# Attention ahead of an expert layer: the gate's product in another set of PSUM banks, the gate's parts one unit later, keys handed to the DMA queue ahead of values

## The chip, the core and the metric

The kernel runs on one core of a Trainium2 chip. The metric is the device time of one execution in microseconds (us). Before the change three runs took 722.42, 722.44 and 722.80 us, median 722.44. The profile shown here is of one further execution, of 717.54 us.

## The reference

Two layers in one kernel. First attention, in 8 batches of 8 heads with 512 local and 32 global positions of width 64: a local query sees the 32 global keys and the local keys at most 32 positions away, a global query sees all 544 keys. Then a mixture of experts over the 4608 resulting rows of 512 numbers, where each of 8 experts takes 576 rows.

```
s_g = scale * q_g @ k_all.T ;  out_g = softmax(s_g) @ v_all
s_l = scale * q_l @ [k_g, k_l].T, local part masked to |i - j| <= 32
out_l = softmax(s_l) @ [v_g, v_l]
x = concat(out_g, out_l) as rows of H * D = 512
logits = x @ w_gate          # 4608 x 8
walk over all (row, expert) in falling order of logits;
    a row goes to the expert if it has none yet and the expert has < 576
out[rows of e] = relu(x[rows] @ w1[e]) @ w2[e]
```

## The kernel before, in words

**Stages.** Attention comes first, then the first expert's choice of its rows (a chain of small steps, nothing beside it), then the eight experts' products, beside which the other experts' choices are made.

**Units.** Attention is a list of 80 units, ten a batch. Two heads make a pair; a batch has pairs 0 to 3, over all batches 0 to 31. A pair has two `Local` units; two pairs together have one `Glob` unit. In batches 0 to 6 the units are four Local, one Glob, four Local, one Glob. In batch 7 they are two Local, both Glob, six Local, so that the second Glob (units[73]) needs the keys of pair 31.

**Steps of a unit.** `a` (L164, L230) multiplies queries and keys into PSUM tile `S` (three banks). `e` masks and takes row maxima on VectorE (DVE, L171, L173) and exponentials on ScalarE (ACT, L176). `c` transposes on TensorE (PE, L181, L259) into PSUM tile `T` (three banks), and `evac` copies the result to SBUF, on ACT (L289) or DVE (L291) by a fixed turn of five. `d` multiplies with the values into PSUM tile `O` (two banks: L193, L269), and DVE divides (L196 to L202, L272 to L276) into the batch's rows `xs` or `xg`. That makes eight banks.

**Order.** The scheduler is off; each engine runs in the order of the code. Step i of the main loop does `c` of unit i, `a` and `e` of unit i+2, `d` of unit i-2. At an even step the order is a, c, gate parts, e, d; at an odd step d, c, gate parts, a, e. So the `d` of an even step and that of the odd step after it come close together.

**Gate.** The logits of batch b are made during the next batch, in six parts: four times four transposes into a T bank (`gate_x`, L297), one product with the gate's weights into an O bank (`gate_m`, L303, placed straight behind `d`), whose result is copied to `ltc`, and four transposes of that into a T bank with a sum on DVE (`gate_l`, L312, L313). The table `GS` gives the steps, counted from an even one. Batches 3 and 7 have another, smaller gate for the global rows.

**DMA queue.** All attention loads and stores go through SyncE's queue (SP) in program order. `slot`, called twice a step, issues one of: a load of a pair's queries and keys (`load_qk`: `q` 272 KB, then `qk` 432 KB), half a pair's values (`load_v`, 520 KB), a store of a quarter of a batch's rows (`stores`, 256 KB), ahead of which the small stores of a Glob's rows go (`late`, four of 8 KB). Ahead of each stands a DMA of four bytes (`pace`) that reads a result of DVE, so the queue cannot run ahead of the computation. A load of keys comes up when its pair is at most three past that of the unit two steps ahead. GpSimd (POOL) copies `q` into the padded tile `qz` (L87), from which `a` reads.

**First choice.** `rt.setup` for the first 24 columns of logits is spread over the last steps of attention, one piece a step, from step nu - 9 on (nu = 80).

Of the kernel before, what the change touches and what calls it, by code (L numbers as in the profile page):

```python
# [8 lines left out]
F32 = mybir.dt.float32  # L9
# [30 lines left out]
@with_exitstack  # L40
def block(ctx, tc, A, out, nbatch=B, dump=None):
    nc = tc.nc
    ctx.enter_context(tc.manual_schedule())
    consts = ctx.enter_context(tc.tile_pool(name="consts", bufs=1))
    dram = ctx.enter_context(tc.tile_pool(name="dram", bufs=1, space=DRAM))
    xd = dram.tile([N, DM], F32, name="xd")
    pace = dram.tile([1, 256], F32, name="pace")

    ident = consts.tile([128, 128], F32, name="ident")
    L = consts.tile([128, 34, E], F32, name="L")  # L50
    if dump is not None:
        nc.vector.memset(L, 0.0)
    rt = Routing(tc, A, consts, L, ident) if out is not None else None
    if rt:
        rt.begin(ctx)
    attention(tc, A, consts, xd, pace, ident, L, nbatch, rt)
    if dump is not None:
        nc.sync.dma_start(dump["L"], L.rearrange("p a b -> p (a b)"))
        nc.sync.dma_start(dump["x"][:nbatch * S], xd[:nbatch * S])
    if out is not None:  # L60
        rt.begin_ps(ctx)
        experts(tc, A, xd, ident, rt, out)
# [3 lines left out]
def attention(ctx, tc, A, consts, xd, pace, ident, L, nbatch, rt=None):  # L66
    nc = tc.nc
# [3 lines left out]
    ps = ctx.enter_context(tc.tile_pool(name="ps", bufs=2, space=PSUM))  # L71
# [4 lines left out]
    def load_qk(b, p):  # L76
        t = ld.tile([128, KW], F32, name="qk", bufs=5)
        q = ld.tile([128, QW], F32, name="q", bufs=3)
        z = qz[(b * NP + p) % NZ]
        nc.sync.dma_start(q, A["qk"][b, p, :, :QW])  # L80
        nc.sync.dma_start(t, A["qk"][b, p, :, QW:])
        qk[b, p] = t

        def spread(eng):
            for h in range(2):
                r = slice(64 * h, 64 * h + 64)
                eng.tensor_copy(z[r, :, h, :], q[r].rearrange("p (j i) -> p j i", i=32))  # L87
        return spread

    def load_v(b, p, h=None):  # L90
        if not h:
            vw[b, p] = ld.tile([128, 2, NW, D + 1], F32, name="vw", bufs=6)
        t = vw[b, p].rearrange("p h w d -> p (h w d)")
        n = NW * (D + 1)
        q = slice(0, 2 * n) if h is None else slice(h * n, h * n + n)
        nc.sync.dma_start(t[:, q], A["vw"][b, p, :, q])
# [5 lines left out]
    P = [(b, p) for b in range(nbatch) for p in range(NP)]  # L102
# [20 lines left out]
    seen, late, stores = [], [], []  # L123
    nl = [3, 4]
    npace = [0]

    def behind():
        nc.sync.dma_start(pace[:, npace[0]:npace[0] + 1], seen[-1])
        npace[0] += 1

    def slot(i):
        v = nl[1] < 2 * nl[0]
        k = not v and nl[0] < len(P) and nl[0] <= pairidx(units[min(max(i, 0) + LA, nu - 1)]) + 3
        if not (v or k or late or stores):
            return
        if i >= 0 and seen:
            behind()
        while late:
            late.pop(0)()
        if stores and (len(stores) > 2 or not v):  # L140
            stores.pop(0)()
        elif v:
            load_v(*P[nl[1] // 2], nl[1] % 2)
            nl[1] += 1
        elif k:
            load_qk(*P[nl[0]])(nc.gpsimd)
            nl[0] += 1

    class Local:
        def __init__(s, b, u):  # L150
# [135 lines left out]
    def evac(dst, src, act=None):  # L286
        nev[0] += 1
        if nev[0] % 5 < 3 if act is None else act:
            nc.scalar.activation(dst, src, AF.Copy)  # L289
        else:  # L290
            nc.vector.tensor_copy(dst, src)  # L291
# [6 lines left out]
        evac(xt[:, c, :n * 128], t[:, :n].rearrange("p a b -> p (a b)"))  # L298

    def gate_m(xt, n):  # L300
        lt = ps.tile([128, 512], F32, name="O", bufs=2)
        for c in range(4):
            nc.tensor.matmul(lt[32 * c:32 * c + 32, :n * 128], wg[:, c, :], xt[:, c, :n * 128],  # L303
                             start=True, stop=True)
        ltc = wk.tile([128, 512], F32, name="ltc", bufs=2)
        evac(ltc[:, :n * 128], lt[:, :n * 128])
        return ltc
# [8 lines left out]
    def gate_units(b, src, J, n):  # L316
        xt = []

        def go(c):
            if c == 0:  # L320
                xt.append(wk.tile([128, 4, 128 * n], F32, name=f"xt{n}", bufs=2))
            if c < 4:
                gate_x(src(), xt[0], c)
            elif c == 4:
                xt.append(gate_m(xt[0], n))
            else:
                gate_l(xt[1], J, n)
        return [lambda c=c: go(c) for c in range(6)]
# [55 lines left out]
    units = []  # L384
# [6 lines left out]
            us = loc[:2] + gl + loc[2:]  # L391
        units += us
    extra, turns, wide = {}, {}, {}
    GS = (0, 2, 4, 6, 8, 9)
    for b in range(nbatch):
        last = b == nbatch - 1
        s0 = 10 * (b + 1) + 1
# [7 lines left out]
        else:  # L405
            for k, f in enumerate(lo):
                (wide if k == 4 else turns).setdefault(s0 + 1 + (k if b == nbatch - 2 else GS[k]), []).append(f)
            if gl:
# [4 lines left out]
    def pairidx(u):  # L413
        if isinstance(u, Local):
            return u.b * NP + u.q
        return u.b * NP + 2 * u.g + 1

    nu = len(units)
    first = rt.setup(slice(0, 24), True) if rt else None
    LA = 2  # L420
    for i in range(-LA, nu + 3):
        if rt and i == 2:
            rt.load()
        if rt and i == 12:
            rt.prepare()
        slot(i)
        even = i % 2 == 0
        if not even and 2 <= i <= nu + 1:
            units[i - 2].d()
            for f in wide.get(i, []):  # L430
                f()
        if even and i + LA < nu:
            units[i + LA].a()
        if 0 <= i < nu:
            units[i].c()
        for f in turns.get(i, []):
            f()
        if not even and i + LA < nu:
            units[i + LA].a()
        if i + LA < nu:  # L440
            units[i + LA].e()
            if i + LA == 0:
                spread1(nc.vector)
            if i >= 0:
                slot(i)
        if even and 2 <= i <= nu + 1:
            units[i - 2].d()
            for f in wide.get(i, []):
                f()
        if i >= nu - 1:  # L450
            while late + stores:
                (late or stores).pop(0)()
        for f in extra.get(i, []):
            f()
        if i >= nu - 1:
            while late + stores:
                (late or stores).pop(0)()
        if rt and i >= nu - 9:
            next(first, None)


# [800 lines left out]
```

## Time and profile before

| stage of the profiled execution | from to, us | PE busy | DVE busy | granted PE clock |
|---|---|---|---|---|
| start of attention | 0 to 20 | 15.96 | 13.00 | 1.00 |
| rest of attention | 20 to 241 | 198.98 | 170.56 | 0.98 |
| first choice of rows | 241 to 274.5 | 11.07 | 25.99 | 0.59 |
| experts | 274.5 to 715.8 | 432.66 | 304.25 | 1.00 |

The profiled execution took 717.54 us, of which 715.8 us are the span from its first to its last instruction. The median of the timed runs is 4.9 us above it. "Busy" is the time in which an engine works on an instruction; the granted clock is a share of full speed (1.00 is 2.4 GHz, 0.50 is 1.2 GHz). In 0 to 215 us the DMA engines are mostly over 80% busy, later much less.

### The profile page before, as it was taken

How to read it: one execution, taken by the hardware profiler on the slowest of the kernel's cores; microseconds unless marked ns; L12 is line 12 of the kernel's file. 1: busy time of each engine (PE TensorE's matmuls, PEld its weight loads, DVE VectorE, ACT ScalarE, POOL GpSimd, SP SyncE). 2: the span in 40 equal slices, each digit the busy share in tenths (PEclk: the TensorE clock that was granted, in tenths of full speed). 3: DMA queues.
4: the chain of work that ended last, by engine and by line, in shares of the span. 5: the costliest groups of instructions: out<-in, count | busy, mean ns of one | idle time of the engine just before them, and what ended most of it. 6: DMA issues, size and time to landing. Idle time of an engine off the chain costs nothing.

```text
span 715.8 us, 20729 instructions
## 1 busy us (share of the span) xinstructions
PE 658.7 (92%) x8182; PEld 554.6 (77%) x8182; DVE 513.8 (72%) x2073; ACT 306.6 (43%) x839; POOL 163.2 (23%) x202
## 2 busy tenths in 40 slices
PE   7989999988969528999999999999999999999996
PEld 6766776866847417977987987987987997998985
DVE  6887888877848777888997898897987872540510
ACT  4646666765636203333442432433443352541511
POOL 5222121321120004024024133223122222411011
PEclk9999999999989858999999999999999999999999
DMA  9978888898882117025235233533514324513001
GB/s 356 387 273 286 299 309 297 307 328 268 314 272 73 61 46 253 1 93 160 109 123 162 79 127 103 174 126 111 199 57 161 149 63 151 195 36 146 16 20 44
DMA packets 37243, 120.49 MB, mean 168 GB/s; under 512 B 7834, under 2 KB 8090, under 8 KB 32794
## 3 DMA queue, kind: packets, MB, share of 16 engines
q1 hardware_dynamic: 26506, 66.73, 26.2%
q0 software_dynamic: 10640, 52.44, 21.3%
q8 instruction: 64, 1.05, 0.6%
q14 instruction: 33, 0.27, 0.1%
HBM read 101.32 MB, written 17.83 MB: 166 GB/s over the span
## 4 chain that ended last, share of the span: by engine, by line
PE 67%; DVE 13%; DMA 11%; ACT 4%; issue 3%; SPq 1%; POOL 0%; POOLq 0%; DVEq 0%; ACTq 0%
PE H L1104 25%; PE Y L1130 24%; DMA vw<-in_vw_dram 4%; DVE p L171 3%; PE S L164 3%; PE R L592 3%; DMA qk<-in_qk_dram 2%; PE H L930 2%; PE Y L1120 2%; ACT p L176 2%; PE T L181 2%; DMA q<-in_qk_dram 1%; PE O L193 1%; PE S L230 1%; DMA w2r<-in_w_dram,widx 1%
## 5 line engine op out<-in xcount | busy, mean ns | idle before, releaser
L1104 PE MATMUL H<-xh,w1h 128*128 128x272 f32 (+2 forms) x512 | 149.9, 293 | 0.7 <-ACT xh L903 0.6
L1104 PE MATMUL H<-xh,w1l 128*128 128x272 f32 (+2 forms) x512 | 150.1, 293 | 0.3 <-DVE w1l L517 0.3
L1104 PE MATMUL H<-xl,w1h 128*128 128x272 f32 (+2 forms) x512 | 148.5, 291 | 0.3 <-DVE xl L517 0.2
L176 ACT ACTIVATE p<-p,nm 128x128 f32<-128x128 f32 x256 | 81.8, 392 | 66.8 <-DVE nm L173 44.6
L1130 PE MATMUL Y<-w2h,hh 128*128 128x512 f32 x256 | 104.1, 407 | 0.0
L1130 PE MATMUL Y<-w2h,hl 128*128 128x512 f32 x256 | 103.3, 403 | 0.0
L1130 PE MATMUL Y<-w2l,hh 128*128 128x512 f32 x256 | 103.2, 403 | 0.0
L1107 ACT ACTIVATE hh<-H 128x272 fp32r<-128x272 f32 (+2 forms) x128 | 50.7, 397 | 115.3 <-PE H L1104 109.8
L1104 PEld LDWEIGHTS H<-xh,w1h 128*128 128x128 f32 x512 | 97.2, 190 | 1.5 <-ACT xh L903 1.0
L1104 PEld LDWEIGHTS H<-xh,w1l 128*128 128x128 f32 x512 | 97.0, 189 | 0.9 <-DVE w1l L517 0.5
L1104 PEld LDWEIGHTS H<-xl,w1h 128*128 128x128 f32 x512 | 96.3, 188 | 1.0 <-DVE xl L517 0.8
L87 POOL COPY qz<-q 64x544 f32<-64x544 f32 x60 | 38.2, 636 | 158.1 <-DMA q<-in_qk_dram 123.7
L164 PE MATMUL S<-qk,qz 128*64 128x128 f32 x1024 | 68.4, 282 | 5.4 <-DVE qz L87 2.8
L517 DVE SCALAR_TENSOR_TENSOR hl<-H,hh 128x272 fp32r<-128x272 f32 (+2 forms) x128 | 55.0, 435 | 20.7 <-ACT h L1109 14.3
L171 DVE CUSTOM_DVE_ANT_0 p<-S,mask 128x128 f32<-128x128 f32 x256 | 59.0, 286 | 14.1 <-PE S L164 7.5
L164 PEld LDWEIGHTS S<-qk,qz 128*64 128x64 f32 x1024 | 56.9, 139 | 11.9 <-issue 4.0
L517 DVE TENSOR_TENSOR w2l<-w2r,w2h 128x512 fp32r<-128x512 f32 x64 | 41.9, 686 | 31.1 <-ACT w2h L903 30.6
L890 POOL DMA_INDIRECT xg<-xd,idx x40 | 39.8, 994 | 101.6 <-DVE idx L517 41.0
L1066 ACT ACTIVATE y<-Y 128x512 f32<-128x512 f32 x32 | 19.1, 598 | 94.9 <-PE Y L1130 80.0
L1130 PEld LDWEIGHTS Y<-w2h,hh 128*128 128x128 f32 x256 | 48.3, 189 | 10.3 <-issue 1.6
L1130 PEld LDWEIGHTS Y<-w2h,hl 128*128 128x128 f32 x256 | 48.3, 189 | 9.2
L1130 PEld LDWEIGHTS Y<-w2l,hh 128*128 128x128 f32 x256 | 48.4, 189 | 8.9
(183 smaller groups left out, 1142.5 us busy)
## 6 DMA issues: line engine op xcount, KB each, us to landing
vw<-in_vw_dram SPq DMA_DIRECT2D x60, 520.0 KB
qk<-in_qk_dram SPq DMA_DIRECT2D x32, 432.0 KB
q<-in_qk_dram SPq DMA_DIRECT2D x32, 272.0 KB
xd<-xs SPq DMA_DIRECT2D x32, 256.0 KB
vw<-in_vw_dram SPq DMA_DIRECT2D x2, 1040.0 KB
pace<-nm SPq DMA_DIRECT2D x83, 0.0 KB
xd<-xg SPq DMA_DIRECT2D x64, 8.0 KB
pace<-ls SPq DMA_DIRECT2D x42, 0.0 KB
```

The costliest lines, as they stand in the source:

```text
L87: eng.tensor_copy(z[r, :, h, :], q[r].rearrange("p (j i) -> p j i", i=32))
L164: nc.tensor.matmul(st[64 * r:64 * r + 64, c, :], z[:, j].rearrange("p h i -> p (h i)"), kw[:, k0:k0 + 128], start=True, stop=True)
L171: nc.vector.tensor_tensor_reduce(s.p[:, c, :], st[:, c, :], mask[:, 4 * s.u + c, :], 1.0, -BIG, ALU.add, ALU.max, nm[:, c:c + 1])
L176: nc.scalar.activation(s.p[:, c, :], s.p[:, c, :], AF.Exp, bias=nm[:, c:c + 1], scale=SCALE)
L181: nc.tensor.transpose(t[:, c, :], s.p[:, c, :], ident)
L517: return op(*args, **kw)
L592: s.nc.tensor.matmul(out, *args, **kw)
L890: nc.gpsimd.indirect_dma_start(out=dst, out_offset=None, in_=src, element_offset=off, in_offset=bass.IndirectOffsetOnAxis(ap=idx, axis=0))
L1066: nc.scalar.activation(y[:n], p[:n], AF.Copy)
L1104: nc.tensor.matmul(p, w[d][:, fs], x[:, d, q], start=(k == 0), stop=(k == 11))
L1107: nc.scalar.activation(hh[:, f, q], p, AF.Relu)
L1130: nc.tensor.matmul(p, h[:, f, q], w[f], start=(f + k == 0), stop=(f + k == 9))
```

## The change

The gate's product takes a T bank in place of an O bank. The steps of the gate's parts in batches 0 to 5 go up by one (the last by one too), so the transposes and the product stand at odd steps; those of batches 6 and 7 stay. `slot` issues a load of keys first whenever one is due; only then a store (if more than two wait, or no values are due), then values. The first choice's setup begins one step later.

```
     def slot(i):
         v = nl[1] < 2 * nl[0]
-        k = not v and nl[0] < len(P) and nl[0] <= pairidx(units[min(max(i, 0) + LA, nu - 1)]) + 3
+        k = nl[0] < len(P) and nl[0] <= pairidx(units[min(max(i, 0) + LA, nu - 1)]) + 3
...
-        if stores and (len(stores) > 2 or not v):
+        if k:
+            load_qk(*P[nl[0]])(nc.gpsimd)
+            nl[0] += 1
+        elif stores and (len(stores) > 2 or not v):
             stores.pop(0)()
         elif v:
             load_v(*P[nl[1] // 2], nl[1] % 2)
             nl[1] += 1
-        elif k:
-            load_qk(*P[nl[0]])(nc.gpsimd)
-            nl[0] += 1
...
     def gate_m(xt, n):
-        lt = ps.tile([128, 512], F32, name="O", bufs=2)
+        lt = ps.tile([128, 512], F32, name="T", bufs=3)
...
-    GS = (0, 2, 4, 6, 8, 9)
+    GS = (1, 3, 5, 7, 9, 10)
...
-        if rt and i >= nu - 9:
+        if rt and i >= nu - 8:
```

On PE, around the gate's product of batch 0 (steps 20 to 22; `xt` are the transposed rows, `wg` the gate's weights, `pgt` a Glob's transposed exponentials):

```order
 L193 MATMUL O<-vw,pt 32x65 x16
-L303 MATMUL O<-xt_880,wg 32x512 x4
 L269 MATMUL O<-vw,pgt 32x64 x24
-L181 MATMUL T<-ident,p 128x128 x4
-L312 MATMUL T<-ident,ltc 128x128 x4
+L303 MATMUL T<-xt_944,wg 32x512 x4
+L181 MATMUL T<-ident,p 128x128 x4
 L164 MATMUL S<-qk,qz_100 64x128 x8
 L230 MATMUL S<-qk,qz_99 64x512
```

Before, three fillings of O follow each other, with the product in the middle; now the two of `d` do, and the product behind them fills a T bank, its transposes (L312) a step later.

On PE, around a later part of the next batch's gate (steps 24 and 25; `xs` are a batch's rows, `pg` a Glob's exponentials):

```order
 L164 MATMUL S<-qk,qz_101 64x128 x16
 L259 MATMUL T<-ident,pg_103 128x128 x6
+L193 MATMUL O<-vw,pt 32x65 x32
+L181 MATMUL T<-ident,p 128x128 x4
 L297 MATMUL T<-ident,xs 128x128 x4
-L193 MATMUL O<-vw,pt 32x65 x32
-L181 MATMUL T<-ident,p 128x128 x4
 L164 MATMUL S<-qk,qz_102 64x128 x16
```

The four transposes of a gate part move from ahead of the two `d` to behind the following `c`, still ahead of the next `a`.

On SP, where batch 5's rows are stored and the keys of pair 29 are loaded (`xs` a batch's rows, `q` and `qk` queries and keys, `vw` values), first before, then after:

```order
L207 DMA xd_62<-xs_3307 128x512
L128 DMA pace_63<-nm_3956 1x1
L207 DMA xd_62<-xs_3307 128x512
L128 DMA pace_63<-nm_3956 1x1
L207 DMA xd_62<-xs_3307 128x512
L128 DMA pace_63<-nm_3980 1x1
L207 DMA xd_62<-xs_3307 128x512
L128 DMA pace_63<-ls_4034 1x1
L80 DMA q_4040<-in_qk_dram 128x544
L81 DMA qk_4039<-in_qk_dram 128x864
```

```order
L80 DMA q_3919<-in_qk_dram 128x544
L81 DMA qk_3918<-in_qk_dram 128x864
L128 DMA pace_63<-nm_3961 1x1
L207 DMA xd_62<-xs_3300 128x512
L128 DMA pace_63<-nm_3961 1x1
L207 DMA xd_62<-xs_3300 128x512
L128 DMA pace_63<-nm_3985 1x1
L96 DMA vw_4015<-in_vw_dram 128x1040
L128 DMA pace_63<-ls_4034 1x1
L80 DMA q_4040<-in_qk_dram 128x544
L81 DMA qk_4039<-in_qk_dram 128x864
L128 DMA pace_63<-nm_4081 1x1
```

Pair 29's keys stand where the first of four stores stood, and two of the stores are pushed back.

On SP, a little later, just ahead of the keys of pair 31 (the last two rows of each; `xg` a Glob's rows), first before, then after:

```order
L280 DMA xd_62<-xg_4166 32x64 x4
L96 DMA vw_4173<-in_vw_dram 128x1040
L128 DMA pace_63<-ls_4192 1x1
L96 DMA vw_4173<-in_vw_dram 128x1040
L128 DMA pace_63<-ls_4192 1x1
L80 DMA q_4220<-in_qk_dram 128x544
L81 DMA qk_4219<-in_qk_dram 128x864
```

```order
L280 DMA xd_62<-xg_4161 32x64 x4
L207 DMA xd_62<-xs_3300 128x512
L128 DMA pace_63<-ls_4186 1x1
L207 DMA xd_62<-xs_3300 128x512
L128 DMA pace_63<-ls_4186 1x1
L80 DMA q_4220<-in_qk_dram 128x544
L81 DMA qk_4219<-in_qk_dram 128x864
```

Pair 31's keys keep their place behind the same set of transfers; the two stores now stand where the two halves of pair 30's values stood, and those have moved ahead of the small stores.

## Rows read from the trace of the kernel before

**Rows 1.** Busy time by stage (us; engine busy (instructions); clock; DMA share; GB/s):

```profile
20.00:241.00 221.00, 198.98 (x4402) 156.60 (x4401) 170.56 (x918) 133.64 (x414) 42.09 (x70) 0.98 0.79 276
241.00:274.50 33.50, 11.07 (x226) 8.09 (x225) 25.99 (x99) 2.79 (x5) 5.38 (x6) 0.59 0.20 61
274.50:715.80 441.30, 432.66 (x3346) 376.76 (x3346) 304.25 (x997) 161.62 (x395) 106.10 (x107) 1.00 0.33 114
```

**Rows 2.** Waits of PE, 55 to 240 us (total us, times, longest):

```profile
PE O L269 <- DVE gm L272: 5.6, 4, 1.8
PE S L230 <- POOL qz L87: 5.1, 1, 5.1
PE O L269 <- ACT p L176: 1.7, 1, 1.7
PE O L193 <- DVE xs L202: 1.2, 1, 1.2
PE O L193 <- DVE xg L276: 1.2, 1, 1.2
PE O L269 <- DVE xs L202: 0.9, 1, 0.9
```

**Rows 3.** Timelines of PE, DVE, ACT, 117 to 122.6 us (start, length, [idle before]):

```profile
118.30 1.04 PE L303 MATMUL O<-xt,wg 128*32 128x512 f32 x8
121.02 0.88 PE L269 MATMUL O<-vw,pgt 128*32 128x64 f32 x48 [1.68 <-ACT p L176]
...
120.44 0.42 DVE L202 TENSOR_TENSOR xs<-O,ls 128x256 f32<-128x256 f32 x1
...
120.24 1.28 ACT L176 ACTIVATE p<-p,nm 128x128 f32<-128x128 f32 x4 [1.15 <-DVE ls L196]
```

**Rows 4.** Busy time from one such wait to the next (PE, PEld, DVE, ACT, POOL):

```profile
121.02:147.87 26.85, 25.03 (x568) 19.95 (x569) 21.66 (x120) 17.32 (x55) 6.14 (x11) 1.00 0.86 306
...
sum 136.34, PE 126.60 PEld 100.16 DVE 109.42 ACT 87.70 POOL 26.19; mean PE 25.32 PEld 20.03 DVE 21.88 ACT 17.54 POOL 5.24
```

**Rows 5.** Timeline of SP's queue, 188.5 to 212 us:

```profile
189.51 0.34 SPq L207 DMA_DIRECT2D xd<-xs  x1
...
193.39 0.35 SPq L80 DMA_DIRECT2D q<-in_qk_dram  x1
...
198.25 4.39 SPq L280 DMA_DIRECT2D xd<-xg  x4
...
204.90 0.35 SPq L80 DMA_DIRECT2D q<-in_qk_dram  x1
```

**Rows 6.** Timelines of PE and POOL, 195 to 217 us:

```profile
203.18 0.97 PE L269 MATMUL O<-vw,pgt 128*32 128x64 f32 x48 [1.11 <-DVE gm L272]
...
211.23 1.11 PE L230 MATMUL S<-qk,qz 128*64 128x512 f32 x3 [5.05 <-POOL qz L87]
...
209.84 1.33 POOL L87 COPY qz<-q 64x544 f32<-64x544 f32 x2 [5.36 <-DMA q<-in_qk_dram]
```

**Rows 7.** Windows of 3 us, 189 to 207 us (last columns: clock, DMA share, GB/s):

```profile
189.00:192.00 3.00, 3.00 (x104) 2.58 (x100) 2.35 (x16) 2.24 (x7) 0.00 (x0) 1.00 0.37 134
192.00:195.00 3.00, 3.00 (x40) 2.08 (x33) 2.73 (x14) 1.37 (x5) 0.00 (x0) 1.00 0.85 278
...
198.00:201.00 3.00, 3.00 (x61) 2.22 (x64) 2.13 (x12) 2.24 (x8) 0.26 (x1) 1.00 1.00 349
201.00:204.00 3.00, 1.89 (x72) 0.99 (x60) 2.30 (x10) 2.35 (x10) 0.79 (x2) 1.00 0.69 189
204.00:207.00 3.00, 2.17 (x18) 1.05 (x10) 0.58 (x2) 0.75 (x2) 0.48 (x1) 1.00 0.80 248
```

**Rows 8.** Clock after two waits of PE: windows, and PE's timeline at 46 us:

```profile
210.00:220.00 10.00, 8.77 (x120) 6.99 (x122) 4.49 (x22) 3.06 (x11) 2.54 (x5) 0.68 0.37 128
...
45.00:50.00 5.00, 3.85 (x38) 3.35 (x42) 3.36 (x18) 3.11 (x12) 2.14 (x5) 0.66 0.97 364
...
46.15 1.98 PE L164 MATMUL S<-qk,qz 128*64 128x128 f32 x16 [2.31 <-ACT pg L248]
```

## The prediction, made before the changed kernel ran

> **What bounds the kernel now.** I read the stages first. The experts keep PE busy for 432.66 of 441.30 us at full clock, and the first choice of rows before them is a chain on DVE with PE mostly idle [rows 1]. No line of the change issues anything there, so I leave both at their length. What can move is attention, 241 us.
>
> There I read PE's waits next, since PE is busy for 198.98 of 221 us [rows 1]. Between 55 and 240 us they have two causes worth counting. One repeats: PE waits before filling an O bank, 4 + 1 + 1 + 1 + 1 = 8 times, 5.6 + 1.7 + 1.2 + 1.2 + 0.9 = 10.6 us [rows 2]. The other comes once: 5.1 us for the copy of queries of the last pair [rows 2].
>
> The timeline shows what the first is. At 118.30 the gate's product (L303) fills an O bank right behind a `d`; the next `d` (L269) would need the bank that the `d` before the product filled, and DVE empties that one only at 120.44 to 120.86 (L202), because the maxima of the unit two steps ahead stand before it in DVE's order. PE starts at 121.02, after 1.68 us [rows 3]. So with only two O banks, a third filling in a row meets DVE's lag. It happens once a batch, and twice in one.
>
> How near is the next limit? Over five stretches from one such wait to the next, 136.34 us long, PE is busy for 126.60 and DVE for 109.42 us; per stretch 25.3 and 21.9 of 27.3 [rows 4]. PE is the fuller engine and idles 1.9 us a stretch, which is nearly all this wait (10.6 / 8 = 1.3 us each, up to 1.8). DMA is at a share of 0.86 and 306 GB/s in one of them [rows 4]; it reaches 1.00 and 349 GB/s elsewhere [rows 7]. So PE leads, with DVE and DMA some 10 to 20% behind.
>
> **The change part by part.**
>
> *The product in a T bank, and the gate at odd steps.* No instruction is added or taken out; L303 keeps its columns. The wait's cause goes: the two fillings of O by `d` now follow each other, and the first of them finds a bank emptied two steps ago. For batches 0 to 5 this comes from the bank and the step together, for batch 6 and the small gate from the bank alone. The most it can give is the 10.6 us. What is late next is DVE: it was behind by the whole wait each time, and stays behind. PE next meets it at the transposes of the following units, which need exponentials that ACT ends at 120.24 + 1.28 = 121.52 [rows 3], about when the wait ended. DVE's idle time per stretch, 27.3 - 21.9 = 5.4 us, has to absorb what PE no longer grants it; a stretch of 27.3 - 1.3 = 26.0 still leaves it 4.1 us, but that idle time also holds its own waits for ACT. So I take two thirds of the wait as gained, 7.0 us, between 0 (every wait comes back at a transposes' bank or an exponential) and 10.6. Below nothing would need T banks to be short: three of them serve the product, and the one it takes was last filled three fillings earlier, two steps back, so I exclude more than a few tenths.
>
> The moved transposes (L297) come behind the next `c` rather than ahead of `d`; they are the same work on PE, and DVE's maxima at even steps are no longer behind their copy. I count nothing for it; it is part of why I do not go below two thirds.
>
> *Keys ahead of values and stores.* In the steady part PE does not wait for keys [rows 2], so nothing is gained there. It matters once, in batch 7, where units[73] wants pair 31 early. Its queries are issued at 204.90 [rows 5], the copy starts at 209.84, and PE resumes at 211.23 after 5.05 us [rows 6]. The burst begins with the first store at 189.51 [rows 5]. In the new order the same transfers stand between that place and pair 31: four stores, pairs 29 and 30, values of 29 and 30, the small stores. So only holes in the DMA's work can be filled. Against 349 GB/s [rows 7] the windows lack (349 - 134) x 3 us = 0.65 MB, (349 - 278) x 3 = 0.21, (349 - 189) x 3 = 0.48 and (349 - 248) x 3 = 0.30 MB: 1.64 MB or 4.7 us. The first two holes (2.5 us) come from the stores, which are issued one at a time, 256 KB each, some 1.0 us apart (193.39 - 189.51 over four) [rows 5]; with 704 KB of keys in the first place I take them as filled. The other two (2.2 us) follow the four small stores, which hold SP for 4.39 us [rows 5]; with both halves of pair 30's values issued ahead of these I take half, 1.1. That is 3.6 us sooner. Against it, PE arrives 1.1 us sooner, since the wait at 203.18 (1.11 us) [rows 6] lies inside this stretch. The wait becomes 5.05 + 1.1 - 3.6 = 2.6 us, a gain of 2.5. Bounds: no hole filled, a loss of 1.1; all filled, a gain of 3.6. Earlier gains move both PE and the paced queue and cancel, as long as DMA keeps up.
>
> *The clock after that wait.* In 210 to 220 us the granted clock averages 0.68 [rows 8], so 6.4 us at the lower level (1.2 GHz), 1.2 of them before PE resumes: 5.2 us of work at half speed, 2.6 us lost. A wait of 2.31 us at 46 us also ended with the lower level: 0.66 over 5 us, 3.4 us of it [rows 8], nearly all after PE resumed at 46.15, so some 1.6 us lost. I take the second price for the shorter wait: a gain of 1.0, between 0 and 2.6. The wait of 1.68 us on an O bank that ended at 121.02 was followed by a clock of 1.00 [rows 3, 4], so I count those waits at their length alone.
> The Trainium skill ("TensorE: Matmul & The Clock Gate", section "Loop structure matters more than you think") says that copying a result out of PSUM beside dense matmuls leaves the clock up, while a long wait for a DMA ahead of them drops it. The trace agrees at these two places. By that rule the loss of 2.6 us stays for as long as PE has to wait for the DMA here, and the sum would be 1.0 us less.
>
> *The rest.* At the start the keys of pairs 3 and 4 go ahead of the values of pair 2; from pair 5's keys on the order there is the old one again. PE's longest wait between 20 and 55 us, 2.31 us at 46 us, is for ACT and not for a load [rows 8], so I count 0, within half a us either way. The setup's pieces one step later are the same DVE work, 0.
>
> Sum: 7.0 + 2.5 + 1.0 = 10.5 us. On the profiled execution 717.54 - 10.5 = 707.0. The timed median stands 4.9 us above it, for a reason that the profile does not show; I take the gain off the median: 722.44 - 10.5 = 711.9 us. Ends of the terms: 10.6 + 3.6 + 2.6 = 16.8 (705.6 us), and 0 - 1.1 + 0 = -1.1 (723.5 us).
>
> **The rivals.**
>
> *DVE takes the wait over.* PE runs ahead, but each batch waits for exponentials or for S banks, and only three tenths of the 10.6 us (3.2) come back. For it: DVE is late at every one of these places [rows 3]. Against: 5.4 us a stretch in which it is not busy [rows 4]. With the tail as forecast: 722.4 - 3.2 - 2.5 - 1.0 = 715.7 us.
>
> *The last batch's wait stays.* No hole is filled, since the queue's bytes ahead of pair 31 are the same: 722.4 - 7.0 + 1.1 = 716.5 us. For it: in 198 to 201 us DMA is already saturated [rows 7]. Against: the four windows with holes.
> The Trainium skill ("DMA: Bandwidth & Descriptors", section "Queues, rings and completion order") says that each DMA engine takes the descriptors of one issuer's queue in their order, so what stands ahead of the keys is moved first whatever it is. No run here shows the rings themselves; by that rule alone this rival's 716.5 would be the time.
>
> *More than forecast.* All of the 10.6 us, all the holes and a clock that does not fall: 722.4 - 16.8 = 705.6 us.
>
> *Slower: the loads become the bound.* If DMA cannot move more per us than it did (306 GB/s per stretch, rows 4), pair 31 lands no earlier than before however early PE is there, and the seven waits before it, 10.6 - 1.2 = 9.4 us, only lengthen the wait at 211.23; what stays is two thirds of the last one, 0.8 us. Now the two stores ahead of pair 31 are issued only as pair 30's values land, so its keys can be behind by a further hole like that of 201 to 207 us (2.2 us) plus the time of one store (0.9, estimated as 256 KB at 306 GB/s): 722.4 - 0.8 + 2.2 + 0.9 = 724.7 us. It decides from where the copy at 209.84 would start later than 212.1, that is 0.8 + 1.44 us later. Against: DMA shares of 1.00 at 349 GB/s [rows 7] while the mean is 0.86.
>
> *The change does nothing:* if the `d` behind L193 still waited for DVE without the product between, 722 us.
>
> **How the numbers follow.** Forecast 0.45 (711.9; its own range 708 to 715, with the first term between a half and nine tenths of 10.6, the second between 1.5 and 3.5, the third between 0.5 and 1.5); DVE takes over 0.19; the last wait stays 0.18; more than forecast 0.08; loads the bound 0.07, 0.03 of it near 722 and 0.04 near 725; nothing 0.03. Faster by over 0.2% (below 721.0; about what a measurement of this kernel tells from no change) 0.90, within it 0.06, slower 0.04. The range 705 to 719 leaves out the last two cases and the far ends of the others.
>
> **What would show it.** Waits of PE on O: gone from between L303 and L269 or L193; if instead T L181 or S L164 wait for DVE or ACT by about a us a batch, DVE has taken over. The batch stretches: 26.0 us instead of 27.3 on average. The wait of L230 for POOL: near 2.6 us; unchanged 5 to 6 with DMA windows full is the second rival, over 12 the fourth. The clock after it: lower level for some 3 us. The forecast is wrong if the batches stay at 27 us or if the experts' 441 us change.

## The result, and the profile after

The change makes the kernel slower: 726.59 us median (20 runs, 720.69 to 731.06) against 722.23 us (20 runs, 718.09 to 725.57). The ratio is 1.0064, with a 95% interval from 1.0042 to 1.0087. Forecast were 711.9 us, and 0.90 for faster.

The profiled execution after took 726.99 us. Its stages answer to [rows 1]; the cuts are put where the same counts of PE instructions fall:

```profile
20.00:250.00 230.00, 206.96 (x4402) 157.62 (x4400) 167.80 (x918) 132.50 (x414) 40.65 (x68) 0.97 0.78 265
250.00:284.00 34.00, 11.24 (x227) 8.23 (x228) 26.26 (x101) 2.79 (x5) 5.64 (x6) 0.59 0.23 73
284.00:725.00 441.00, 433.95 (x3346) 378.08 (x3346) 304.27 (x996) 162.57 (x395) 105.97 (x107) 0.99 0.33 113
```

First choice and experts keep their length. Attention takes 250 instead of 241 us. These 9 us are more than the change costs (726.59 - 722.23 = 4.4 us by the medians): 726.99 us is near its median, the profiled execution before (717.54 us) lay 4.9 us under its own. Waits of PE and of DVE, 55 to 250 us, against [rows 2]:

```profile
PE S L230 <- POOL qz L87: 8.5, 1, 8.5
PE T L181 <- ACT p L176: 2.3, 5, 0.6
PE T L181 <- ACT pgt L289: 2.1, 3, 1.0
```

```profile
DVE p L171 <- DMA pace<-nm: 16.4, 11, 2.7
...
DVE xs L202 <- DMA pace<-ls: 1.7, 1, 1.7
```

The waits on O banks are gone, as forecast. The wait for pair 31 is 8.5 us instead of 5.1. DVE has a wait that it hardly had before (0.9 us in all in 20 to 240 us; 18.6 us now): it may not overwrite a unit's `nm` or `ls` until the queue has read four bytes of it, and the queue is late. The timeline of PE and DVE at the place of [rows 3]:

```profile
119.41 0.86 PE L269 MATMUL O<-vw,pgt 128*32 128x64 f32 x48
...
120.08 1.04 PE L303 MATMUL T<-xt,wg 128*32 128x512 f32 x8
...
121.29 0.29 DVE L171 CUSTOM_DVE_ANT_0 p<-S,mask 128x128 f32<-128x128 f32 x1 [1.56 <-DMA pace<-nm]
```

PE goes from `d` into the product without a pause, while DVE stands still for the queue until 121.29 us, 1.56 us long. Where the loads stand is seen at the end of attention. SP's timeline, 194 to 217 us, against [rows 5]:

```profile
194.23 4.28 SPq L280 DMA_DIRECT2D xd<-xg  x4
...
198.93 0.35 SPq L80 DMA_DIRECT2D q<-in_qk_dram  x1
...
210.84 2.24 SPq L280 DMA_DIRECT2D xd<-xg  x4
213.59 0.98 SPq L207 DMA_DIRECT2D xd<-xs  x1
...
215.33 0.34 SPq L207 DMA_DIRECT2D xd<-xs  x1
...
216.10 0.35 SPq L80 DMA_DIRECT2D q<-in_qk_dram  x1
```

The last row is pair 31's queries: 216.10 instead of 204.90. Windows of 3 us over the two groups of small stores and stores, against [rows 7]:

```profile
198.00:201.00 3.00, 3.00 (x32) 1.94 (x31) 2.73 (x16) 1.98 (x6) 0.00 (x0) 1.00 0.42 104
213.00:216.00 3.00, 0.00 (x0) 0.00 (x0) 0.00 (x0) 0.00 (x0) 0.00 (x0) 0.89 0.42 145
```

Both are holes, that is, stretches in which the DMA engines have little to move (104 and 145 GB/s), and the second lies in front of pair 31 while PE does nothing. Pair 31's copy and PE's restart, against [rows 6], and the clock after it, against [rows 8]:

```profile
219.10 1.33 POOL L87 COPY qz<-q 64x544 f32<-64x544 f32 x2 [8.83 <-DMA q<-in_qk_dram]
```

```profile
220.49 1.11 PE L230 MATMUL S<-qk,qz 128*64 128x512 f32 x3 [8.53 <-POOL qz L87]
```

```profile
216.00:226.00 10.00, 5.51 (x32) 4.19 (x32) 1.20 (x4) 1.83 (x7) 2.20 (x4) 0.52 0.66 221
220.49:230.00 9.51, 9.51 (x128) 7.66 (x130) 4.74 (x22) 3.31 (x12) 1.37 (x3) 0.73 0.34 121
```

PE resumes 9.3 us later than before, at the lower clock. The same stretch before, from PE's restart on:

```profile
211.23:220.00 8.77, 8.77 (x120) 6.98 (x122) 4.49 (x22) 3.06 (x11) 1.37 (x3) 0.70 0.29 100
```

So PE works at the lower level for (1 - 0.73) x 2 x 9.51 = 5.1 us after the restart, as against (1 - 0.70) x 2 x 8.77 = 5.3 us before (the two levels being shares of 1.00 and 0.50).

### The profile page after: what moved, and what is told of

The parts are those of the page before. It is cut to its first block, busy times and chain, and to the rows that moved or that the text cites. A ratio compares the mean times of both kernels' runs of the same rounds, so it can differ in the third digit from the quotient of the medians.

```text
span 725.2 us, 20747 instructions
## 1 busy us (share of the span) xinstructions
PE 669.1 (92%) x8182; PEld 558.0 (77%) x8182; DVE 510.0 (70%) x2073; ACT 306.4 (42%) x839; POOL 163.3 (23%) x202
## 4 chain that ended last, share of the span: by engine, by line
PE 75%; DVE 10%; DMA 9%; issue 2%; ACT 2%; SPq 1%; POOL 0%; POOLq 0%; DVEq 0%; ACTq 0%
PE H L1104 26%; PE Y L1130 23%; PE S L164 5%; DMA pace<-nm 4%; PE T L181 3%; PE R L592 3%; PE O L193 3%; PE H L930 2%; DMA vw<-in_vw_dram 2%; PE Y L1120 2%; DVE p L171 2%; PE S L230 1%; PE T L259 1%; PE T L297 1%; DMA xg<-xd,idx 1%
## 5 line engine op out<-in xcount | busy, mean ns | idle before, releaser
L171 DVE CUSTOM_DVE_ANT_0 p<-S,mask 128x128 f32<-128x128 f32 x256 | 58.8, 285 | 34.2 <-DMA pace<-nm 18.6
L181 PE MATMUL T<-ident,p 128*128 128x128 f32 x256 | 51.1, 298 | 5.4 <-ACT p L176 3.2
```

Source lines behind the costliest of these rows:

```text
L171: nc.vector.tensor_tensor_reduce(s.p[:, c, :], st[:, c, :], mask[:, 4 * s.u + c, :], 1.0, -BIG, ALU.add, ALU.max, nm[:, c:c + 1])
L181: nc.tensor.transpose(t[:, c, :], s.p[:, c, :], ident)
```

## The experiments

There are four groups of four kernels. Each group has its own runs of the kernel before (medians 722.82, 724.33, 723.39 and 724.28 us). A ratio is against those, with its 95% interval in brackets. Traces are of one execution each.

### Which part of the change costs, and is it the pacing?

**The change with the queue's old order** (the hunk in `slot` is taken back, the rest of the change stays):

```
-        k = nl[0] < len(P) and nl[0] <= pairidx(units[min(max(i, 0) + LA, nu - 1)]) + 3
+        k = not v and nl[0] < len(P) and nl[0] <= pairidx(units[min(max(i, 0) + LA, nu - 1)]) + 3
...
-        if k:
+        if stores and (len(stores) > 2 or not v):
...
```

> The change with the old order in the load queue (product in a T bank, gate at odd steps, setup a step later; keys behind stores and values again). Theory A, the early keys put two stores and the small stores behind the values, so that the queue falls behind and VectorE waits for the four-byte pacing reads of its maxima: VectorE's waits for those reads are back near 1 us (0.9 us before, 18.6 us in the change), the last wait of TensorE for pair 31 is 4 to 7 us, time 712 to 717 us. Theory B, TensorE without the waits on the O banks simply outruns the queue, whatever its order: the waits for the pacing reads stay above 10 us and the time is 722 us or more.

721.52 us, ratio 0.9994 [0.9964, 1.0024]. Neither theory came out whole: DVE's waits for the pacing reads of its maxima fall to 3.3 us (20 to 240 us), nearly as A has it, and the time stays near 722 us, as B has it. **The new order alone** (that hunk put into the kernel before, nothing else of the change):

> The kernel before with the new order in the load queue alone (product in an O bank, gate at even steps). Theory A: VectorE waits for pacing reads 8 us or more, the last wait for pair 31 is about 8 us as in the change, and the O-bank waits are still there, so it is the slowest of all: 726 to 734 us. Theory B: pacing waits below 3 us since TensorE is still held at the O banks; 720 to 725 us.

726.67 us, ratio 1.0046 [1.0018, 1.0073]. The time is in A's range, its signs are not: DVE waits 5.9 us for the pacing reads of its maxima and PE 5.6 us for pair 31 (55 to 250 us), and the kernel is no slower than the change. So the order of the queue makes the loss: (1.0064 - 0.9994) x 723 = 5 us with the gate's part and (1.0046 - 1) x 723 = 3 us without, 2 to 3 us either way. The gate's part gives nothing that can be told from noise, though the waits on O banks are gone in the first and there in the second. Is DVE's wait for the pacing reads the cause? **The change, and the kernel before, with more buffers for what those reads read:**

```
-            s.nm = wk.tile([128, NB], F32, name="nm", bufs=4)
+            s.nm = wk.tile([128, NB], F32, name="nm", bufs=8)
-            ls = wk.tile([128, 2, 2], F32, name="ls", bufs=4)
+            ls = wk.tile([128, 2, 2], F32, name="ls", bufs=8)
```

> The change with eight buffers in place of four for the row maxima and the sums that the pacing reads read, so that VectorE no longer has to wait for a read of four units back. Theory A in its narrow form (the pacing reads are what costs): the 18.6 us of VectorE's waits go to under 2 us, time 710 to 718 us, with the last wait for pair 31 still 8 us or more. Theory C, the loads themselves are the bound and the pacing read only shows it: the waits move to TensorE waiting for copied queries or values, time within 2 us of the change (725 to 729 us).

> The kernel before with eight buffers for the same two tiles, nothing else. All theories: its one wait of VectorE for a pacing read is 0.9 us, so the time is within 1.5 us of the kernel before. If it is faster by 3 us or more, the pacing reads cost the kernel before as well in a way that its wait table does not show.

726.92 us, ratio 1.0053 [1.0028, 1.0077]; and 721.92 us, ratio 0.9985 [0.9961, 1.0009]. The times stayed. In the first the wait only changed its name; DVE's waits, 55 to 250 us:

```profile
DVE xs L202 <- DMA xd<-xs: 10.8, 4, 5.3
```

DVE now waits for rows' stores that are late in the same queue. The pacing shows the queue's lateness and does not make it.

### Keys, values and stores

**Stores first, then keys, then values.** The change makes two swaps at once: keys ahead of values, and keys ahead of stores. This keeps the first only:

```
-        if k:
+        if stores and (len(stores) > 2 or not v):
+            stores.pop(0)()
+        elif k:
             load_qk(*P[nl[0]])(nc.gpsimd)
             nl[0] += 1
-        elif stores and (len(stores) > 2 or not v):
-            stores.pop(0)()
```

> The change, but a store goes ahead of keys whenever more than two wait (or no values are due), as in the kernel before; only keys and values have changed places. Theory 'stores behind the keys cost it' (the two stores that stand just ahead of pair 31 make the hole): those stores move forward again, the wait of L230 for POOL falls from 8.5 to about 5 us and the time to about 722 us, ratio 0.998 to 1.002. Rival 'keys ahead of values cost it' (values arrive late, the queue is held longer at each key): the time stays near 726.5 us, ratio 1.005, and the wait stays over 7 us.

719.64 us, ratio 0.994 [0.992, 0.9961]: faster than the change and than the kernel before, and better than expected. The stores behind the keys cost (1.0064 - 0.994) x 723 = 9 us. Its trace has still 6.8 us of wait for pair 31, so more than the tail is cured: `e` of units[64] (the scaling of its maxima on DVE) comes at 182.6 us instead of 186.1, that of units[79] at 237.7 instead of 243.7.

**The same order without the gate's part** (this `slot` in the kernel before):

> The kernel before with keys ahead of values only: stores keep their place ahead of both, the gate's product and steps are the old ones. Theory 'the loads bound it, and keys are the loads that come late': this gains by itself what the change with stores first gained, ratio 0.992 to 0.997. Rival 'the gain needs the gate's new bank and steps as well': ratio 0.998 to 1.002.

721.82 us, ratio 0.9981 [0.9956, 1.0006], not told from no change; keys ahead of values give little without the gate's part. Stores behind keys cost (1.0046 - 0.9981) x 723 = 5 us there.

**The kernel before, once more:**

> The kernel before, unchanged, for a second trace. Theory 'the loads bound attention in most executions, and the profiled one was a lucky one': this one takes 721 to 726 us and shows waits for loads (PE's S for keys or their copy, some 4 to 7 us in all in 85 to 160 us) that the first does not have. Rival 'the profile always shows that picture, and timed runs are longer for another reason': 717 to 719 us and no such waits.

723.19 us, and the theory holds, as far as one further execution shows it. Waits of PE, 55 to 245 us:

```profile
PE S L230 <- POOL qz L87: 5.6, 1, 5.6
...
PE S L164 <- DMA pace<-nm: 3.2, 1, 3.2
PE S L164 <- POOL qz L87: 2.4, 1, 2.4
```

The last two were not in the execution that I predicted from [rows 2]. They are 5.6 us together, and this execution is 723.19 - 717.54 = 5.7 us longer than that one. That the two agree so closely is luck: the waits on O banks are also smaller here (7.5 against 10.6 us), and the clock falls once more (0.96 over 100 to 140 us, 1.00 in the first).

### With less to load

The values of a batch's fourth pair are not loaded (an eighth of the traffic), in the kernel before, in the change, and in the change with the old order:

```
     def load_v(b, p, h=None):
+        if p == 3:
+            vw[b, p] = vw[b, 2]
+            return
```

> The kernel before, without loading the values of each batch's fourth pair (it multiplies with those of the third): one eighth of a batch's traffic, 1.04 MB of some 8.1 MB, is left out, all else stays. Theory 'the loads bound attention in most runs': at some 290 GB/s this frees 3.6 us a batch, so attention falls back to PE's own pace with the waits on O banks in it; 712 to 718 us, ratio 0.986 to 0.994. Rival 'PE and DVE bound the batches, the loads only the last wait': only the tail gains, 718 to 721 us, ratio 0.994 to 0.999.

> The change, with the same traffic left out (the values of each batch's fourth pair). Theory 'the loads bound it': with room in the queue the waits on O banks pay as first forecast, so this is 5 to 10 us below the light kernel before (705 to 711 us), and the order of the queue costs nothing any more. Rival 'DVE or ACT take the waits over' (the O banks were never worth anything): within 2 us of the light kernel before.

> The change with the old order of the queue, and the same traffic left out. Theory 'the loads bound it, and the order only tells when they are short': within 2 us of the light change, 5 to 10 us below the light kernel before. Rival 'the new order costs by itself': 3 to 5 us below the light change.

710.85, 707.18 and 709.46 us; ratios 0.9814 [0.9784, 0.9844], 0.9768 [0.9734, 0.9802], 0.9801 [0.9772, 0.983]. The loads bound it: 13 us come back in the kernel before, more than expected. Not all of them are in the steady part: `e` of units[72] comes at 203.0 us, and in the kernel before at 202.1 (profiled execution) and 207.8 (the second one); the wait for pair 31 behind it is gone. The new order costs nothing here: the old one is 2.3 us above it, about 3 either way. But the change gains only 3.7 us on its light counterpart, also about 3 either way, fewer than the 5 to 10 expected. The traces tell where the rest is: `e` of units[72] comes at 203.0 (before), 194.0 (change) and 195.3 us (old order), 9.0 and 7.7 us sooner, and then PE of the light change waits for pair 31, 55 to 250 us (lines are three higher here):

```profile
PE S L233 <- POOL qz L87: 7.4, 1, 7.4
```

The O banks pay up to there, and the last pair takes most of it back.

### The last pair, and the small stores

**Pair 31's keys behind those of pair 30**, ahead of values (on the kernel with stores first; `...` stands for the rest of the line):

```
-        k = ... <= pairidx(units[min(max(i, 0) + LA, nu - 1)]) + 3
+        k = ... <= pairidx(units[min(max(i, 0) + LA, nu - 1)]) + 3 + (nl[0] == len(P) - 1)
```

> The change with stores first, and the keys of the last pair (31) come up one pair sooner, that is right behind those of pair 30 and ahead of the values of pairs 29 and 30, which landed over 20 us before their use. Theory 'at the end of attention it is the place of pair 31 in the queue, not the sum of the bytes, that PE waits for': the wait of L230 falls from 6.8 to under 2 us and the time by 5 to 8 us, to 711 to 715 us, ratio 0.983 to 0.989. Rival 'the bytes bound it': the wait moves to the values or to the next keys and the time stays within 2 us of the change with stores first.

712.11 us, ratio 0.9844 [0.9803, 0.9884], as expected; PE's wait for that copy is gone from the trace.

**The four small stores as one**, on top of it. Around them the queue stalls. SP's timeline of the change, 131 to 141 us, and the windows there:

```profile
132.78 0.33 SPq L96 DMA_DIRECT2D vw<-in_vw_dram  x1
134.69 0.24 SPq L128 DMA_DIRECT2D pace<-nm  x1
134.99 2.86 SPq L280 DMA_DIRECT2D xd<-xg  x4
138.41 0.22 SPq L128 DMA_DIRECT2D pace<-ls  x1
138.73 0.35 SPq L80 DMA_DIRECT2D q<-in_qk_dram  x1
```

```profile
135.00:137.00 2.00, 2.00 (x33) 1.18 (x30) 1.86 (x12) 1.80 (x6) 1.27 (x2) 1.00 1.03 404
137.00:139.00 2.00, 1.96 (x83) 1.38 (x72) 1.35 (x7) 1.72 (x5) 0.00 (x0) 1.00 0.63 237
139.00:141.00 2.00, 2.00 (x20) 1.21 (x21) 1.77 (x15) 0.94 (x4) 0.00 (x0) 1.00 0.56 147
```

From the last half of values (132.78) to the next keys (138.73), 6 us, SP hands over 32 KB and some pacing reads; the DMA engines work off what was there and fall to 0.56. What the queue waits for at that line (55 to 250 us, change):

```profile
SPq L280 <- DMA qk<-in_qk_dram: 10.5, 11, 1.7
```

These are landings of keys whose data the small stores do not use. The edit:

```
-                for r in range(4):
-                    nc.sync.dma_start(ap_of(xd, b * S * DM + (4 * g + r) * D, [[DM, SG], [1, D]]),
-                                      xg[32 * r:32 * r + 32, :])
+                nc.sync.dma_start(ap_of(xd, b * S * DM + 4 * g * D, [[D, 4], [DM, SG], [1, D]]), xg)
```

> The same, and the four small stores of a Glob's rows are one DMA. Theory 'the small stores hold the queue until earlier transfers land, and make a hole each time' (each of the four waits on the landing of an earlier transfer): SP's time on that line falls from 2.3 to 4.3 us each to under 1.5, and the time by 2 to 5 us more. Rival 'the holes cost nothing, since values land 10 us and more ahead': within 1 us of the kernel without this.

698.94 us, ratio 0.9671 [0.9629, 0.9713]: 13 us more, far above the 2 to 5 expected, and the fastest kernel here. Its windows, 60 to 140 us, above those of the kernel before:

```profile
60.00:100.00 40.00, 39.85 (x880) 31.66 (x868) 33.47 (x183) 27.21 (x88) 7.31 (x12) 1.00 0.94 336
100.00:140.00 40.00, 39.23 (x903) 31.73 (x902) 34.75 (x190) 27.36 (x86) 10.01 (x17) 1.00 0.90 312
```

```profile
60.00:100.00 40.00, 36.25 (x815) 28.06 (x807) 31.10 (x168) 25.25 (x82) 7.19 (x12) 1.00 0.85 295
100.00:140.00 40.00, 38.32 (x868) 31.09 (x857) 34.21 (x185) 26.49 (x83) 8.79 (x15) 1.00 0.87 306
```

So the DMA engines can take more than the 0.85 and 295 GB/s of before. This kernel differs from before in gate and order too; the kernel before with one small store alone, below, reaches 0.92 and 331 GB/s in the first of these stretches.

### The forecast's terms without that bound

One small store in the kernel before, in the change, and in the change with the old order; and the fastest kernel with the gate's product back in an O bank at the old steps:

```
-        lt = ps.tile([128, 512], F32, name="T", bufs=3)
+        lt = ps.tile([128, 512], F32, name="O", bufs=2)
...
-    GS = (1, 3, 5, 7, 9, 10)
+    GS = (0, 2, 4, 6, 8, 9)
```

> The kernel before with the four small stores of a Glob's rows as one DMA, nothing else. Theory 'these stores hold the loads back, and the loads bound attention': 710 to 716 us, ratio 0.981 to 0.991, with PE's waits on O banks in it and the waits for keys gone. Rival 'the small stores only mattered with the keys of pair 31 early': 720 to 723 us, ratio 0.996 to 1.001.

> The change with the four small stores as one DMA. Theory 'with room in the queue the O banks pay': at the last batch (the unit 72 steps in) this is 7 to 10 us ahead of the kernel before with one small store, as in the light kernels (194.0 against 203.0 us); at the end 3 to 9 us ahead, since the wait for pair 31 takes part of it back: 703 to 711 us. Rival 'the new order of the queue costs as much with one small store as with four': 714 us or more, no better than the kernel before with one small store.

> The change with the old order of the queue, and the four small stores as one DMA. Theory 'the order costs only where transfers are short of time, now mostly at pair 31': 1 to 4 us below the same with the new order. Rival 'the new order costs 5 us whatever else': 5 us or more below. If keys ahead of values are worth something by themselves, it lies above.

> The kernel that was fastest so far (stores first, then keys, then values; pair 31's keys early; one small store; 698.94 us), with the gate's product back in an O bank at the old steps. Here neither the loads nor the last pair are waited for, so the O banks' term stands alone. Theory 'the 10.6 us of waits on O banks are real and pay in full once nothing else bounds': 7 to 11 us above, 706 to 710 us. Rival 'DVE takes two thirds or more of it back': up to 4 us above, at most 703 us.

The four, in this order:

- The kernel before with one: 708.56 us, ratio 0.9783 [0.9759, 0.9807], better than expected.
- The change with one: 704.27 us, ratio 0.9739 [0.9707, 0.9771], as expected.
- The change with one, old order: 703.67 us, ratio 0.9714 [0.9678, 0.9749].
- The fastest with the gate as before: 708.37 us, ratio 0.9781 [0.9759, 0.9803], as the theory has it.

At units[72] the change with one is 201.6 - 197.5 = 4.1 us ahead of the kernel before with one, fewer than the 7 to 10 expected; with the old order it is 201.6 - 192.1 = 9.5 us ahead. The last figure flatters: that profiled execution (700.25 us) lies 3.4 us under its median, the other two within 0.7 us of theirs. SP spends 0.53 us on the one store; the kernel before with one, SP at 126.79 us, and the windows there and at the next such store (138.82 us):

```profile
126.79 0.53 SPq L279 DMA_DIRECT2D xd<-xg  x1
```

```profile
126.00:128.00 2.00, 2.00 (x58) 1.64 (x46) 1.75 (x7) 2.00 (x9) 0.68 (x2) 1.00 1.01 328
138.00:140.00 2.00, 2.00 (x46) 1.66 (x46) 1.96 (x11) 1.25 (x5) 0.81 (x2) 1.00 1.00 361
```

The holes at these places are gone.

In the last kernel PE's waits on O banks are back, 55 to 235 us, 4.0 + 1.5 + 1.2 + 1.2 = 7.9 us:

```profile
PE O L269 <- DVE gm L272: 4.0, 4, 1.2
PE O L193 <- DVE xg L276: 1.5, 1, 1.5
...
PE O L269 <- ACT p L176: 1.2, 1, 1.2
PE O L193 <- DVE xs L202: 1.2, 1, 1.2
```

Its distance to the fastest is (0.9781 - 0.9671) x 724 = 8 us, with about 3 either way. All ratios by order of the queue (from the four groups, each against its own runs of before):

| gate | small stores | old order | stores, keys, values | keys, stores, values (the change) | stores, keys, values, pair 31 early |
|---|---|---|---|---|---|
| old | four | 1 | 0.9981 | 1.0046 | not run |
| old | one | 0.9783 | not run | not run | 0.9781 |
| new | four | 0.9994 | 0.9940 | **1.0064** | 0.9844 |
| new | one | 0.9714 | not run | 0.9739 | **0.9671** |

With one small store the gate's part is worth (0.9783 - 0.9714) x 724 = 5 us in the old order, and the new order costs (0.9739 - 0.9714) x 724 = 2 us, about 3 either way in both: the second cannot be told from nothing. In the traces the new order still loses 197.5 - 192.1 = 5.4 us by units[72], 3.4 us of which may be the execution profiled. The change as a whole then gains (0.9783 - 0.9739) x 724 = 3 us, also about 3 either way.

## Why the prediction was wrong

**The step that failed** is the sentence that PE leads "with DVE and DMA some 10 to 20% behind", and what hangs on it: that earlier gains "cancel, as long as DMA keeps up". I read a DMA share of 0.86 as 14% of room. This queue could not give it to a faster PE: with the gate's part and the old order `e` of units[72] comes at 206.2 us with four small stores and at 192.1 with one. With less to load the kernel before gains 13 us, with one small store for four 16 us, and its share rises to 0.92 over 60 to 100 us in the latter:

```profile
60.00:100.00 40.00, 36.48 (x826) 28.24 (x818) 30.99 (x170) 25.64 (x82) 8.82 (x14) 1.00 0.92 331
```

In the profiled execution of the kernel before the queue did not yet hold PE back ahead of the last batch: units[72] comes at 202.1 us there and hardly sooner with one small store (201.6). Against it the gain is the wait for pair 31 and what follows it; the second execution (207.8 us) has some 6 us of it ahead of units[72] as well. The rows to read were SP's own waits, which I never put beside those of PE; in the kernel before, 55 to 240 us:

```profile
SPq L280 <- DMA vw<-in_vw_dram: 10.7, 11, 1.8
...
SPq L280 <- DMA qk<-in_qk_dram: 4.2, 6, 1.2
```

**The O banks (7.0 us forecast).** The waits went, and the size was right where nothing else bounds: 8 and 5 us with one small store, about 3 either way. In the kernel as it is they gave nothing (0.9994), since a PE that is sooner waits for the same loads. The rival in which DVE takes the wait over (3.2 us) fits the 5 as well, but not the 8; in the fastest kernel PE waits for neither exponentials nor S banks in 55 to 235 us. DVE's new waits in the change are for the queue.

**Keys ahead (2.5 us forecast).** Here the sign was wrong, for two reasons. At the end of attention I counted the holes that keys would fill in 189 to 195 us ("I take them as filled"). The two stores that moved went beside the small stores, and both places became holes. Pair 31's queries go out at 216.10 us, against 210.20 with the gate's part and the old order:

```profile
210.20 0.35 SPq L80 DMA_DIRECT2D q<-in_qk_dram  x1
```

The wait became 8.5 us instead of 2.6 (before 5.1 and 5.6 us in the two executions).

The second reason is larger, as far as single executions near their medians show it. I took the order as worth nothing in the steady part, as PE did not wait for keys in that one execution. Against the gate's part with the old order, 209.8 - 206.2 = 3.6 us are lost by units[72] and 243.7 - 239.3 = 4.4 us by units[79]. Without the gate's part, against the second execution of the kernel before, it is 211.7 - 207.8 = 3.9 us of 4.1, and the wait for pair 31 is the same 5.6 us. One place stands out in that trace, on DVE and then on PE:

```profile
152.74 0.29 DVE L171 CUSTOM_DVE_ANT_0 p<-S,mask 128x128 f32<-128x128 f32 x1 [3.19 <-DMA pace<-nm]
```

```profile
155.02 1.51 PE L269 MATMUL O<-vw,pgt 128*32 128x64 f32 x48 [5.72 <-DVE gm L272]
```

Two swaps were in the edit: keys ahead of values helps with the gate's part (0.9994 to 0.9940), stores behind keys costs more than that. Why stores behind keys also lose time in the steady part was not taken apart; holes beside the small stores, as at 139 us, are seen in other batches too, but the cost of each was not measured.

**The clock (1.0 us forecast).** The wait did not shrink, and the lower level lasted 5.1 us after PE's restart, as against 5.3 before: this term gave 0.

**The slower rival (724.7 us, chance 0.07)** named the place and part of the mechanism: two stores ahead of pair 31, issued late, and a copy that starts after 212.1 (219.10). Its time lies 1.9 us under the measured 726.6, and its chance was far too low: "DMA shares of 1.00 at 349 GB/s" stood against it, but a peak of 3 us says nothing of what the queue keeps up over a batch. Its own sign, a wait of over 12 us, did not come (8.5): it let PE arrive early at pair 31, while in the runs PE had already lost that lead to loads and order in the steady part.

**The median 4.9 us above the profiled execution** was in the prediction as "a reason that the profile does not show". It was the clue: the loads come more or less late from execution to execution, as far as two traces show it, and the one shown had no wait for keys before the last pair. Right were the first choice, the experts, and the gate's vanished waits.

## What to carry to other kernels

Where one queue in program order feeds a kernel, a mean DMA share below 1 need not be slack (here 0.85 and 0.86 gave a faster PE nothing): look at what the queue itself waits for, and at the windows around its smallest transfers, before crediting a saving on an engine. When the profiled execution stands below the median, take a second trace before concluding from the first that nothing waits for loads. And when the new order moves transfers of two kinds past each other, price each swap alone.

## What was not expected of the hardware

Four stores of 8 KB in a row held SP for 1.7 to 4.4 us in the kernel before, while one of 32 KB takes some 0.53 us. In the kernel before they cost 16 us of 724 (ratio 0.9783), in the change with the old order (0.9994 - 0.9714) x 724 = 20 us, though they are 32 KB of some 4 MB that attention loads and stores for two pairs. The Trainium skill ("DMA: Bandwidth & Descriptors", section "Rules for kernel authors") says to coalesce many small transfers into one, as under 64 KB it is mostly overhead. The trace agrees on what to do; the store of 32 KB is still under that size, and yet these 16 us came back. In 55 to 240 us of the kernel before the small stores hold SP for 40.5 us, and 10.7 + 4.2 = 14.9 us of this are waits for earlier landings; one store each holds it for 7.5 us, with no wait for a landing. How much of the 16 us comes from the waits, and how much from the three further issues, was not separated.
